# A planner that plays each candidate move forward before it orders TensorE's work

## The chip, the core and the metric

The kernel runs on one core of one Trainium2 chip. A core has engines that run their own instruction streams in order and wait for one another by semaphores: TensorE (PE in the profile; its weight loads are PEld), VectorE (DVE), ScalarE (ACT), GpSimd (POOL) and SyncE (SP, which here issues the DMA transfers). The metric is device time in microseconds (us). "The region" below always means the part of a run between value steps 16 and 448, a term explained with the kernel.

## What is computed

A gated attention block over 2048 tokens of width 640. The input is normalised, goes through attention with 32 heads of width 20, and through a two-layer ReLU network whose output, after a SiLU, gates the attention's output. The input is added at the end.

```python
xn = _layernorm(x, axis=-1)
qkv = (xn @ wqkv)                       # 32 heads, Dh = 20
scores = einsum("bhqd,bhkd->bhqk", q, k) * scale
p = softmax(scores, axis=-1)
s = (einsum("bhqk,bhkd->bhqd", p, v) merged) @ wo
g = silu(relu(xn @ w1) @ w2)
return x + s * g
```

All inputs and the output are fp32.

## The kernel before

**Order written at build time.** The kernel is built with a manual schedule: instructions run on each engine in the order in which the Python program emits them. A `Plan` object (L81 to L154) keeps a simulated clock in nanoseconds: `plan.t` for PE, `plan.free["act"]`, `plan.free["dve"]` and so on for the times at which the other engines come free, with fixed prices at the top of the file (`PAIR` 220 for a pair of score matmuls, `PV` 850 for a value step, `MM` 216 and `MM_HALF` 136 for filling, `EXP` 585, `RED` 605, `LAG` 210 from PE to a reader, `BACK` 120 back to PE). A loop at the end of the program (L1252 to L1301) looks at this clock, picks what PE does next, emits it with all that follows from it, and goes on. The simulated clock serves only to choose the order; the chip runs at its own pace.

**The attention.** Heads are taken four at a time (8 groups `g`), queries 512 at a time (4 columns `c`), keys 128 at a time (16 tiles `k`). That is 8 x 4 x 16 = 512 *value steps*. Work for them comes in units of one 128 x 512 block of scores of one head:

- A *maximum unit* (`mx_unit`, L617): a matmul with queries down the partitions (L629) into a PSUM bank, and a reduction on DVE (L633). After the 64 units of one `(g, c)`, `highest` (L640) and `rows` (L658) transpose the maxima on PE (L661), split them on DVE and send them through DRAM into two extra rows of the queries (`m_d`, one store and four loads on SP), which subtract the maximum inside the second score matmul.
- A *score unit* (`st_unit`, L719): a matmul with keys down the partitions (L732) and an exponential on ACT (L736) into one of three weight buffers (`ring`, `PTS` = 3, four units each).
- A *value step* (`weigh`, L764): when four score units are done, four heads' fp32 matmuls with the values (L772), side by side in PE's columns, into the bank `pv`. After 16 of them `normalise` (L780) copies `pv` out, transposes it on PE (L794), divides and stores it.

Contractions of the two score matmuls have 60 and 62 rows, so two units run side by side in PE's two half arrays: `pair` (L645) emits them two at a time, in the kinds score and maximum, two scores, or two maxima. Seven PSUM banks (`BANKS`) are shared by all this and the filling.

**The filling.** All other matrix products are cut into pieces that may go between: value projections, query and key projections of later heads, the hidden layer (`gate_hidden`, L846), the gate (`gate_out`, L917) and the first four fifths of the output projection (`out_first`, L1019). Each is a generator; `products` (L298) splits a contraction of 128 rows into two halves of 64 so that a filling piece uses the same half-array layout as the pairs (L314), with two accumulations at a time, each in its own bank. Between the two halves it waits until PE's order has read the earlier ones back (`plan.seen > last`). Filling pieces are 512 wide (L314 with tiles `xt`) or 320 wide (`w2`, `v` and `wo`).

Changing between the half-array layout ("A"), the value step's layout ("P") and the full array ("F") costs `SWITCH` in the plan.

**The choice before.** The loop takes the first that applies: a pair whose banks and operands are ready within `STAY`, and whose ACT or DVE queue is shorter than `FULL` (while in layout A) or `SOON` (otherwise), the neediest first; up to two value steps (`pv_count`), if no pair is coming, the queues are longer than `STOCK`, or PE isn't in layout A; a small task (the transposes of `rows` and `normalise`); a piece of the start-up chain (`first`); a piece of filling, if it is behind its pace or no pair is coming. `pace` (L1245) lets filling run `AHEAD` = 40000 ns ahead of a share of `FILLING` (the price of all filling but the output projection, 481 us in the plan's prices) in proportion to value steps done, and without limit after step 448. `mx_start` lets maxima run at most 64 + 160 units ahead of the scores' column.

Of the kernel before, what the change touches and what calls it, by code (L numbers as in the profile page):

```python
# [17 lines left out]
P = 128  # L18
# [7 lines left out]
NT = S // P  # L26
CW = 512
NC = S // CW
TPC = CW // P
NG = H // 4  # L30
# [4 lines left out]
PTS = 3  # L35
BANKS = 7
STEPS = NG * NC * NT
INF = float("inf")
# [10 lines left out]
EPS = 1e-5  # L49


SWITCH = 100
LAG = 210
BACK = 120
PAIR = 220
PV = 850
MM = 216
MM_HALF = 136
TURN = 110
EXP = 585  # L60
RED = 605
# [5 lines left out]
SLACK = 500  # L67
LEAN = 5000
XS = 12
SOON = 560  # L70
STAY = 60
FULL = 1300
MIXED = 400
STOCK = 900
AHEAD = 40000
OTS = 4
FILLING = NT * 15 * MM_HALF * 2 + (KD - 1) * NC * 30 * MM + NC * KF * 15 * MM + NT * 72 * MM_HALF
LEAD = 80


class Plan:  # L81
# [3 lines left out]
    def __init__(self):  # L85
        self.t = 0.0
        self.mode = None
        self.free = dict.fromkeys(("act", "dve", "pool", "dma", "sp"), 0.0)
        self.out = deque()
        self.events = []  # L90
        self.count = 0
        self.idle = 0.0
        self.switches = 0
        self.issued = 0
        self.seen = 0
        self.filled = 0.0
        self.jobs = []
        self.woken = 0.0

    def at(self, when, fn):  # L100
        heappush(self.events, (when, self.count, fn))
# [41 lines left out]
    def begin(self, mode, ready):  # L143
        return max(self.t + (SWITCH if mode != self.mode else 0), ready)

    def pe(self, mode, cost, ready=0.0):

        start = self.begin(mode, ready)
        self.switches += mode != self.mode
        self.idle += start - self.t - (SWITCH if mode != self.mode else 0)  # L150
        self.mode = mode
        self.issued += 1
        self.t = start + cost
        return self.t + LAG  # L154


@with_exitstack
def attention_gate(ctx: ExitStack, tc: tile.TileContext, x, wqkv, wo, w1, w2, out):
    nc = tc.nc
    ctx.enter_context(tc.manual_schedule())  # L160
    plan = Plan()
# [11 lines left out]
    pv = psum.tile([P, CW], F32, name="pv")  # L173
    banks = [psum.tile([P, CW], F32, name=f"ps{i}") for i in range(BANKS)]
    bank_free = [0.0] * BANKS
    behind = [0] * BANKS
# [5 lines left out]
    def take():  # L182

        i = min(range(BANKS), key=lambda i: bank_free[i])
        ready = bank_free[i]
        bank_free[i] = INF
        return i, ready
# [33 lines left out]
    small = []  # L221
# [76 lines left out]
    def products(ps, pairs, free):  # L298

        if st_done[0] == 0 or st_done[0] > 4 * (STEPS - 10):
            return (yield from whole(ps, pairs, free))
        cost = MM if ps[0].shape[-1] == CW else MM_HALF
        half = [slice(0, P // 2), slice(P // 2, P)]
        n = len(pairs[0])
        for second in range(2):
            for i in range(n):
                yield free  # L310
                for which in range(2):
                    rows = half[which ^ second]
                    a, b = pairs[which][i]
                    nc.tensor.matmul(ps[which], a[rows], b[rows],  # L314
                                     start=(i == 0 and not second), stop=(i == n - 1 and bool(second)))
                got = plan.pe("A", cost, free)
            if not second:
                last = plan.issued
                yield from when(lambda: plan.seen > last)
        return got  # L320

    def whole(ps, pairs, free):
# [8 lines left out]

    def take_two():
        (a, fa), (b, fb) = take(), take()
        return (a, b), max(fa, fb)


# [114 lines left out]
    def when(test):  # L451
        while not test():
            yield INF
# [33 lines left out]
    pack_ready = {}  # L487
# [98 lines left out]
    def v_tiles(n, t):  # L586
# [7 lines left out]
        for u, b in zip((t, t + 1), bs):  # L594
# [99 lines left out]
    st_done = [0]  # L694
    pts = {}
    pv_done = [0]
    pv_free = [0.0]
    pt_free = {}
    st_issued = {}
    p_ready = {}  # L700
# [5 lines left out]
    def where(step):  # L706
        return step // (NC * NT), step // NT % NC, step % NT
# [56 lines left out]
    def weigh():  # L764
        step = pv_done[0]
        g, c, k = where(step)
        pv_done[0] += 1
        pt = pts.pop(step)
        plan.seen = max(plan.seen, st_issued.pop(step))
        got = plan.pe("P", PV, max(p_ready.pop(step), pv_free[0] if k == 0 else 0))  # L770
        for h in range(4):
            nc.tensor.matmul(pv[32 * h:32 * h + DH + 1, :], va[g // 4][:, k, 4 * (g % 4) + h, :], pt[:, h, :],  # L772
                             start=(k == 0), stop=(k == NT - 1))
        pt_free[step] = plan.t + BACK
        if k == NT - 1:
            normalise(g, c, got)
# [309 lines left out]
    first = deque()  # L1086
    fill = deque()
# [73 lines left out]
    def values(n):  # L1161
        for t in range(0, NT, 2):
            yield from v_tiles(n, t)
        if n == 0:
            v_half(1)
        else:
            wvp.close()
# [34 lines left out]
    def ready_of(q, many=1):  # L1202


        best = INF, None
        n = 0
        for gen in list(q):
            at = head(q, gen)
            if at is None:
                continue  # L1210
            n += 1
            if at < best[0]:
                best = at, gen
            if best[0] <= plan.t + STAY or n == many:
                break
        return best

    def step_of(q, gen):
        del heads[gen]
        head(q, gen)  # L1220

    log = []

    def starving(engine):
        return plan.free[engine] - plan.t < SOON

# [18 lines left out]
    def pace():  # L1245
# [3 lines left out]
            return AHEAD + FILLING * (1 + n / ((NG - 1) * NC * NT))  # L1249
        return INF  # L1250

    while True:  # L1252
        plan.due()
        t = plan.t
        go = plan.begin("A", 0)
        options = choose(t)
        inside = plan.mode == "A"
        now = [o for o in options if o[0] <= go + STAY and o[1] < (FULL if inside else SOON)]
        if now:
            best = min(now, key=lambda o: (o[1] if len(set(o[2])) == 1 else o[1] - MIXED))  # L1260
            pair(best[2])
            log.append((t, "".join(best[2])))
            continue
        n = pv_count()
        coming = min([o[0] for o in options if o[1] < FULL], default=INF)
        if n and (coming == INF or min(plan.free["act"], plan.free["dve"]) - t > STOCK or plan.mode != "A"):
            for _ in range(n):
# [59 lines left out]
```

## Time and profile before

| | |
|---|---|
| time, median of 3 runs | 1788.44 us (1787.75 to 1790.27) |
| profiled execution | 1788.3 us |
| its span, first to last instruction | 1786.5 us |
| matmul instructions | 14887 |
| score units, maximum units | 2048 each |
| value matmuls (L772) | 4096, in 512 steps of eight |
| granted PE clock, mean | 0.992 |

Busy time of an engine is the union of its instructions' recorded times. Matmuls overlap in the records: a 512-wide one is recorded with some 0.38 us and the next may begin 0.06 or 0.22 us after it, so a busy PE isn't the same as a PE that does all it could. In the timeline the first column is the start, the second the length of a merged run of instructions, and "x16" how many were merged. A row of busy time in a stretch begins with the stretch and its length, then each engine's busy time and number of instructions, the granted PE clock, the DMA engines' share and GB/s; asked for a line or a tile, it holds that line's or tile's instructions alone. In the rows of waits come who waited, for whom, the total in us, how often, and the longest.

### The profile page before, as it was taken

Reading aid. Unit: us, or ns where it says so; the run is one execution under the profiler, and the core shown is the slowest. Engines: PE = TensorE matmul, PEld = TensorE weight load, DVE = VectorE, ACT = ScalarE, POOL = GpSimd, SP = SyncE. Lnnn points to the kernel's source line nnn. Section 1 sums busy time; section 2 is a strip of 40 time slices with the busy share of each in tenths; the row PEclk is TensorE's granted clock in tenths of the full one; section 3 lists DMA queues with packets and bytes.
Section 4 is the critical chain, followed back from the end, with each engine's and each line's share of the span. In section 5 each row is a group of like instructions: output and inputs, shape, how many; then the busy total and the mean of one; then the engine's idle time right before and its main releaser. Section 6 shows DMA issues by size and latency. Waiting matters only on the chain. (4 is left out here: it accounts for less than half of the span.)

```text
span 1786.5 us, 36686 instructions
## 1 busy us (share of the span) xinstructions
PE 1734.0 (97%) x14887; PEld 723.6 (41%) x14887; DVE 1451.6 (81%) x2512; ACT 1390.6 (78%) x2338; POOL 315.9 (18%) x338
## 2 busy tenths in 40 slices
PE   4999999999999999999999989999999999999998
PEld 3443334444332333444433324444444444344332
DVE  7699988888888888888888878888888888887522
ACT  3537788888888888887887868888788878887785
POOL 1631200002111455322221103000000000012221
PEclk8999999999999999999999999999999999999998
DMA  6324311201115332311112071131013100323332
GB/s 240 102 62 125 99 33 35 49 20 37 58 41 162 96 93 89 107 51 43 45 39 73 29 216 42 55 92 56 13 55 92 55 9 20 109 87 124 102 100 74
DMA packets 133995, 135.30 MB, mean 76 GB/s; under 512 B 26640, under 2 KB 110480, under 8 KB 133824
## 3 DMA queue, kind: packets, MB, share of 16 engines
q1 hardware_dynamic: 133248, 131.63, 24.4%
q8 instruction: 116, 1.90, 0.4%
q10 hardware_dynamic: 576, 1.31, 0.2%
q14 instruction: 55, 0.45, 0.1%
HBM read 85.32 MB, written 47.58 MB: 74 GB/s over the span
## 5 line engine op out<-in xcount | busy, mean ns | idle before, releaser
L736 ACT ACTIVATE pt<-ps,cexp 128x512 f32<-128x512 f32 x2048 | 1249.4, 689 | 293.0 <-PE ps L732 244.8
L633 DVE TENSOR_REDUCE m<-ps 128x1 f32<-128x512 f32 x2048 | 1274.4, 684 | 211.0 <-PE ps L629 204.6
L629 PE MATMUL ps<-kp,qp 60*128 60x512 f16 x2048 | 585.6, 378 | 5.3 <-ACT pt L736 3.7
L732 PE MATMUL ps<-qp,kp 62*128 62x512 f16 x2048 | 579.4, 379 | 9.3 <-DVE m L633 4.7
L772 PE MATMUL pv<-pt,va 128*21 128x512 f32 x4096 | 523.0, 600 | 0.0
L732 PEld LDWEIGHTS <-kp 62*128 62x128 f16 x2048 | 147.3, 93 | 332.2 <-issue 289.6
L629 PEld LDWEIGHTS <-qp 60*128 60x128 f16 x2048 | 150.1, 93 | 117.3 <-issue 84.7
L772 PEld LDWEIGHTS pv<-pt,va 128*21 128x21 f32 x4096 | 88.4, 100 | 237.3 <-issue 226.4
L1048 POOL TENSOR_TENSOR pre<-pre,go 128x320 f32<-128x320 f32 x32 | 27.0, 864 | 596.3 <-DVE go L1046 596.3
L314 PE MATMUL ps<-w2th,hh 64*128 64x320 f16 x768 | 126.5, 296 | 0.1
L314 PE MATMUL ps<-w2th,hl 64*128 64x320 f16 x768 | 126.0, 295 | 0.0
L314 PE MATMUL ps<-w2tl,hh 64*128 64x320 f16 x768 | 125.6, 295 | 0.0
L314 PEld LDWEIGHTS <-hh 64*128 64x128 f16 x1536 | 88.2, 94 | 51.2 <-issue 10.5
L314 PE MATMUL ps<-xt_hi,1h 64*128 64x512 f16 x480 | 102.7, 376 | 0.0
L314 PE MATMUL ps<-xt_lo,1h 64*128 64x512 f16 x480 | 102.1, 375 | 0.0
L314 PE MATMUL ps<-xt_hi,1l 64*128 64x512 f16 x480 | 100.3, 375 | 0.5 <-POOL 1l L287 0.5
L314 PEld LDWEIGHTS <-1h 64*128 64x128 f16 x960 | 58.7, 94 | 53.0 <-issue 18.7
L896 POOL CAST hh<-hr 128x512 f16<-128x512 f32 x48 | 29.3, 610 | 287.2 <-ACT hr L894 258.5
L482 POOL TENSOR_TENSOR loq<-rq,hiq 128x512 f16<-128x512 f32 x16 | 18.5, 1159 | 260.2 <-ACT rq L480 260.2
L314 PE MATMUL ps<-xt_hi,qh 64*128 64x512 f16 x150 | 56.4, 376 | 0.0
L314 PE MATMUL ps<-xt_lo,qh 64*128 64x512 f16 x150 | 56.4, 376 | 0.0
L898 POOL TENSOR_TENSOR hl<-hr,hh 128x512 f16<-128x512 f32 x48 | 55.7, 1160 | 3.8
(219 smaller groups left out, 1521.7 us busy)
## 6 DMA issues: line engine op xcount, KB each, us to landing
kp<-k_d SPq DMA_DIRECT2D x28, 240.0 KB
qp<-q_d SPq DMA_DIRECT2D x28, 240.0 KB
hh_d<-hh SPq DMA_DIRECT2D x48, 128.0 KB
hl_d<-hl SPq DMA_DIRECT2D x48, 128.0 KB
hh<-hh_d SPq DMA_DIRECT2D x8, 768.0 KB
hl<-hl_d SPq DMA_DIRECT2D x8, 768.0 KB
q_d<-hiq SPq DMA_DIRECT2D x20, 256.0 KB
k_d<-hik SPq DMA_DIRECT2D x20, 256.0 KB
```

Source lines behind the costliest of these rows:

```text
L314: nc.tensor.matmul(ps[which], a[rows], b[rows], start=(i == 0 and not second), stop=(i == n - 1 and bool(second)))
L482: nc.gpsimd.tensor_sub(lo, r, hi)
L629: nc.tensor.matmul(banks[b], qp[p % RING][r, t:t + P], kp[p % RING][r, kc * CW:(kc + 1) * CW], start=True, stop=True)
L633: nc.vector.tensor_reduce(m4[:, 2 * pr + j, qt, kc:kc + 1], banks[b], axis=AX.X, op=ALU.max)
L732: nc.tensor.matmul(banks[b], kp[p % RING][r, k * P:(k + 1) * P], qp[p % RING][r, c * CW:(c + 1) * CW], start=True, stop=True)
L736: exps[step, u] = nc.scalar.activation(pt[:, u, :], banks[b], AF.Exp, scale=cexp).ins
L772: nc.tensor.matmul(pv[32 * h:32 * h + DH + 1, :], va[g // 4][:, k, 4 * (g % 4) + h, :], pt[:, h, :], start=(k == 0), stop=(k == NT - 1))
L896: nc.gpsimd.tensor_copy(hi, r)
L898: nc.gpsimd.tensor_sub(lo, r, hi)
L1048: nc.gpsimd.tensor_add(pre[:, t, ns], pre[:, t, ns], gts[t][:, ns])
```

## The change

A class `Look` is added: a small copy of the plan's state (PE's time and layout, seven banks, ACT's and DVE's queues, counts of units and steps, the filling piece in hand), with the same prices. In the region, and while some scores and maxima are left (16 and 8 units at least), the loop no longer takes the first choice that applies:

- Small tasks and start-up pieces that are ready go first.
- Otherwise every possible move (`moves`) is tried on a copy, and the old rules (`go_on`) are played on from there; at 4, 5, ... 19 us after the decision the state is scored by `loss`, and the move with the smallest sum is emitted (`best`). Nothing is emitted during the trial.
- `loss` is PE time that did no matmul, a quadratic term for filling away from its target, and 100 ns for each unit by which the maxima's lead over the scores is below 140. The target has `AHEAD` as before; the quadratic term adds `BEHIND` = 60000 ns to the lag, so it is smallest where filling is 60 us below `target`.
- A value step is chosen one at a time. A chosen filling piece may wait up to 1 us for its operand; otherwise filling is not offered for 300 ns. Without any move the plan's clock goes 40 ns on.
- `products` and `take_two` note the filling piece in hand and its two banks, for `Look` to copy.

Before step 16 and after step 448 the old rules run. Two of their constants change, there and in the played moves: `SWITCH` 100 to 120, `SOON` 560 to 700.

```diff
-SWITCH = 100
+SWITCH = 120
...
-SOON = 560
+SOON = 700
...
+HELD = 1e15
+STOCKED = 0.0
+BEHIND = 60000
+FAR = 100
+WANT = 140
+HORIZON = 20000
+FROM = 4000
+SWAY = 2e5
...
+class Look:
...
+    def pe(self, mode, cost, ready):
+        self.t = max(self.t + (SWITCH if mode != self.mode else 0), ready) + cost
+        self.mode = mode
+        self.issued += 1
+        self.useful += cost
...
+    def moves(self):
+        t = self.t
+        res = [o[2] for o in self.options() if o[0] <= t + 300]
+        if self.values():
+            res.append("pv")
+        if self.fill_at() <= t + 300:
+            res.append("fill")
+        return res
+
+    def best(self):
+
+        moves = self.moves()
+        if not moves:
+            return None
+        found = None
+        for move in moves:
+            new = self.copy().make(move)
+            loss = 0
+            for end in range(FROM, HORIZON, 1000):
+                while new.t < self.t + end:
+                    new.go_on()
+                loss += new.loss(self)
+            if found is None or loss < found[0]:
+                found = loss, move
+        return found[1]
+
+    def loss(self, begun):
+        lag = self.filled - self.target(self) + BEHIND
+        return self.t - begun.t - (self.useful - begun.useful) + lag * lag / SWAY - STOCKED * (
+            min(self.act - self.t, 1200) + min(self.dve - self.t, 1200)) + FAR * max(0, WANT - (self.mx - self.st))
...
+    A_STEP = PV + 4 * PAIR
+
+    def target(at):
+
+        done = at.pv * PV + (at.st + at.mx) * PAIR / 2
+        return FILLING * min(1, done / ((NG - 1) * NC * NT * A_STEP)) + AHEAD
...
     while True:
         plan.due()
         t = plan.t
+        assert t < 3e6
+        if 16 <= pv_done[0] < 448 and st_done[0] < 4 * STEPS - 16 and mx_done[0] < len(mx_units) - 8:
+            urgent = [s for s in small if s[0] <= t + STAY]
+            if urgent:
+                small.remove(urgent[0])
+                urgent[0][2]()
+                log.append((t, "small"))
+                continue
+            (a, of_first), (b, of_fill) = ready_of(first, 8), ready_of(fill)
+            if a <= t + STAY:
+                step_of(first, of_first)
+                log.append((t, "first"))
+                continue
+            open_ = b < INF or (plan.part and plan.part["left"] == plan.part["half"])
+            move = look(bool(open_) and t >= blocked).best()
+            if move == "pv":
+                weigh()
+                log.append((t, "pv"))
+                continue
+            if move == "fill":
+                if b < t + 1000:
+                    if b > t:
+                        plan.idle += b - t
+                        plan.t = b
+                        plan.due()
+                    filled = plan.t
+                    step_of(fill, of_fill)
+                    plan.filled += plan.t - filled
+                    log.append((t, "fill"))
+                else:
+                    blocked = t + 300
+                continue
+            if move:
+                pair(("st",) * move[0] + ("mx",) * move[1])
+                log.append((t, "stst" if move[0] > 1 else "stmx" if move[0] else "mxmx"))
+                continue
+            plan.idle += 40
+            plan.t += 40
+            continue
```

`go_on` repeats the old choice step by step on the copy, `make` books a move's prices there, `values` tells how many value steps are ready (not counting whether the projected values are), and `look` copies the state from the plan.

More of the change, by code (lines that the diff above doesn't have):

```diff
@@ L98, in __init__ @@
         self.woken = 0.0
+        self.part = None
+        self.last_part = 15, MM
     def at(self, when, fn):
@@ L154, in pe, with copy, take, options @@
         return self.t + LAG
+class Look:
+    def copy(self):
+        new = Look.__new__(Look)
+        new.__dict__.update(self.__dict__)
+        new.free = self.free[:]
+        new.behind = self.behind[:]
+        new.steps = self.steps.copy()
+        return new
+    def take(self):
+        i = min(range(BANKS), key=self.free.__getitem__)
+        ready = self.free[i]
+        self.free[i] = HELD
+        return i, ready
+    def pe(self, mode, cost, ready):
[3 more added lines that the diff above has]
+        self.useful += cost
+    def options(self):
+        two = sorted(self.free)[1]
+        if two >= HELD:
+            return []
+        st = min(self.st_cap, 4 * (self.pv + PTS)) - self.st
+        mx = min(self.mx_cap, self.st // 64 * 64 + self.lead) - self.mx
+        act, dve = self.act - self.t, self.dve - self.t
+        res = []
+        if st > 0:
+            at = two if self.st < self.st_known else max(two, self.st_next)
+            if mx > 0:
+                res.append((at, max(act, dve), (1, 1)))
+            if st > 1:
+                res.append((at, act, (2, 0)))
+        if mx > 1:
+            res.append((two, dve, (0, 2)))
+        return res
+    def values(self):
+        n = 0
+        while n < 2:
+            step = self.pv + n
+            if 4 * step + 4 > self.st or n and step % NT == 0:
+                break
+            ready = max(self.steps[step][0], self.pv_free if step % NT == 0 else 0)
+            if ready > self.t + (SWITCH if self.mode != "P" else 0) + n * PV + STAY:
+                break
+            n += 1
+        return n
+    def fill_at(self):
+        if not self.can_fill:
+            return INF
+        if self.left == 0 and not self.reserve():
+            return INF
+        if self.left == self.half and not self.seen > self.last:
+            return INF
+        return max(self.t, self.part_free)
+    def reserve(self):
+        if sorted(self.free)[1] >= HELD:
+            return False
+        (a, ra), (b, rb) = self.take(), self.take()
+        self.held = a, b
+        self.part_free = max(ra, rb)
+        self.left = 2 * self.half
+        return True
+    def make(self, move):
+        if move == "pv":
+            ready, issued = self.steps.pop(self.pv)
+            self.seen = max(self.seen, issued)
+            self.pe("P", PV, max(ready, self.pv_free if self.pv % NT == 0 else 0))
+            self.pv += 1
+            if self.pv % NT == 0:
+                if self.act < self.dve:
+                    self.act = max(self.act, self.t + LAG) + 600
+                    self.pv_free = self.act + BACK
+                else:
+                    self.dve = max(self.dve, self.t + LAG) + 690
+                    self.pv_free = self.dve + BACK
+                self.dve += 740
+        elif move == "fill":
+            self.pe("A", self.cost, self.part_free)
+            self.filled += self.cost
+            self.left -= 1
+            if self.left == self.half:
+                self.last = self.issued
+            if self.left == 0:
+                for b in self.held:
+                    self.act = max(self.act, self.t + LAG) + self.evac
+                    self.free[b] = self.act + BACK
+        else:
+            ready = self.st_next if move[0] and self.st + move[0] > self.st_known else 0
+            (a, ra), (b, rb) = self.take(), self.take()
+            self.seen = max(self.seen, self.behind[a], self.behind[b])
+            self.pe("A", PAIR, max(ra, rb, ready))
+            got = self.t + LAG
+            for b, st in ((a, move[0] > 0), (b, move[0] > 1)):
+                if st:
+                    self.act = max(self.act, got) + EXP
+                    self.free[b] = self.act + BACK
+                    self.steps[self.st // 4] = self.free[b], self.issued
+                    self.st += 1
+                else:
+                    self.dve = max(self.dve, got) + RED
+                    self.free[b] = self.dve + BACK
+                    self.mx += 1
+                    if self.mx % 64 == 0:
+                        self.dve += 750
+                self.behind[b] = self.issued
+        return self
+    def go_on(self):
+        t = self.t
+        inside = self.mode == "A"
+        options = self.options()
+        go = t if inside else t + SWITCH
+        best = None
+        for o in options:
+            if o[0] <= go + STAY and o[1] < (FULL if inside else SOON):
+                want = o[1] - MIXED if o[2][0] == 1 else o[1]
+                if best is None or want < best[0]:
+                    best = want, o[2]
+        if best:
+            return self.make(best[1])
+        n = self.values()
+        coming = min([o[0] for o in options if o[1] < FULL], default=INF)
+        if n and (coming == INF or min(self.act, self.dve) - t > STOCK or not inside):
+            for _ in range(n):
+                self.make("pv")
+            return self
+        at = self.fill_at()
+        if at <= t + STAY and (self.filled < self.target(self) or coming > t + MM + 20):
+            return self.make("fill")
+        nxt = min(at, coming)
+        for o in options:
+            if o[1] >= FULL:
+                nxt = min(nxt, t + o[1] - FULL)
+        if self.pv in self.steps and 4 * self.pv + 4 <= self.st:
+            nxt = min(nxt, max(self.steps[self.pv][0], self.pv_free if self.pv % NT == 0 else 0) - STAY - SWITCH)
+        self.t = max(t + 20, nxt if nxt < HELD else t + 100)
+        return self
+    def moves(self):
+        t = self.t
+        res = [o[2] for o in self.options() if o[0] <= t + 300]
[3 more added lines that the diff above has]
+            res.append("fill")
+        return res
+    def best(self):
[17 more added lines that the diff above has]
+            min(self.act - self.t, 1200) + min(self.dve - self.t, 1200)) + FAR * max(0, WANT - (self.mx - self.st))
@@ L307, in products @@
         n = len(pairs[0])
+        plan.part = part = dict(left=2 * n, half=n, last=0, cost=cost, free=free, banks=plan.taken)
         for second in range(2):
@@ L316, in products @@
                 got = plan.pe("A", cost, free)
+                part["left"] -= 1
             if not second:
-                last = plan.issued
+                part["last"] = last = plan.issued
                 yield from when(lambda: plan.seen > last)
+        plan.part, plan.last_part = None, (n, cost)
         return got
@@ L333, in take_two @@
         (a, fa), (b, fb) = take(), take()
+        plan.taken = a, b
         return (a, b), max(fa, fb)
@@ L1250, in pace, with look @@
         return INF
+    A_STEP = PV + 4 * PAIR
+    def target(at):
+        done = at.pv * PV + (at.st + at.mx) * PAIR / 2
+        return FILLING * min(1, done / ((NG - 1) * NC * NT * A_STEP)) + AHEAD
+    def look(can_fill):
+        now = Look()
+        now.t, now.mode = plan.t, plan.mode
+        now.free = [min(f, HELD) for f in bank_free]
+        now.behind = behind[:]
+        now.act, now.dve = plan.free["act"], plan.free["dve"]
+        now.st, now.mx, now.pv = st_done[0], mx_done[0], pv_done[0]
+        now.steps = {k: (p_ready[k], st_issued[k]) for k in range(pv_done[0], (st_done[0] + 3) // 4)}
+        now.pv_free = pv_free[0]
+        now.issued, now.seen = plan.issued, plan.seen
+        now.useful = 0.0
+        now.filled = plan.filled
+        now.target = target
+        now.can_fill = can_fill
+        part = plan.part
+        now.left, now.half, now.cost, now.last, now.part_free = (
+            (part["left"], part["half"], part["cost"], part["last"], part["free"]) if part else (0,) + plan.last_part + (0, 0))
+        now.held = part["banks"] if part else ()
+        now.evac = 480
+        now.lead = 64 + 2 * LEAD
+        now.st_known = now.st_cap = st_done[0]
+        now.st_next = 0.0
+        for n in range(1, 33):
+            unit = st_done[0] + n - 1
+            g, c, k = where(unit // 4)
+            if unit >= 4 * STEPS or (g, c) not in q_ready:
+                break
+            now.st_cap = unit + 1
+            if q_ready[g, c] <= plan.t:
+                now.st_known = unit + 1
+            else:
+                now.st_next = q_ready[g, c]
+        now.mx_cap = mx_done[0]
+        for n in range(1, 41):
+            if mx_done[0] + n > len(mx_units):
+                break
+            g, c, kc, qt, pr, j = mx_units[mx_done[0] + n - 1]
+            p = 2 * g + pr
+            if max(pack_ready.get((p, "k", kc * CW), INF), pack_ready.get((p, "q", c * CW), INF)) > plan.t:
+                break
+            now.mx_cap = mx_done[0] + n
+        return now
+    blocked = 0.0
     while True:
@@ L1254, in attention_gate @@
         t = plan.t
+        assert t < 3e6
[13 more added lines that the diff above has]
+            move = look(bool(open_) and t >= blocked).best()
+            if move == "pv":
+                weigh()
[11 more added lines that the diff above has]
+                    log.append((t, "fill"))
+                else:
+                    blocked = t + 300
[7 more added lines that the diff above has]
+            continue
         go = plan.begin("A", 0)
```

## The prediction

> **What bounds the kernel now.** I read the page's busy table first, then the timeline of PE over 10 us, then busy time by source line in chosen stretches, and last who waited for whom.
>
> ```profile
> span 1786.5 us, 36686 instructions
> PE 1734.0 (97%) x14887; PEld 723.6 (41%) x14887; DVE 1451.6 (81%) x2512; ACT 1390.6 (78%) x2338; POOL 315.9 (18%) x338
> ```
>
> PE looks full, which would leave the change some 3%. But the busy time of pipelined matmuls overlaps and hides gaps, so I rebuild PE's load from distances between starts.
>
> ```profile
> 1251.38 1.91 PE L772 MATMUL pv<-pt,va 128*21 128x512 f32 x16
> 1253.23 0.39 PE L732 MATMUL ps<-qp,kp 62*128 62x512 f16 x2
> 1253.45 0.38 PE L629 MATMUL ps<-kp,qp 60*128 60x512 f16 x2
> 1253.77 1.06 PE L772 MATMUL pv<-pt,va 128*21 128x512 f32 x8
> 1254.76 0.39 PE L732 MATMUL ps<-qp,kp 62*128 62x512 f16 x1
> ...
> 1258.65 0.33 PE L314 MATMUL ps<-w2th,hh 64*128 64x320 f16 x2
> 1258.79 0.32 PE L314 MATMUL ps<-w2tl,hh 64*128 64x320 f16 x2
> ```
>
> The reader sees four prices. A pair of 512-wide half-array matmuls lasts 0.216 us (1253.23 to 1253.45 shows 0.22), a 320-wide pair 0.136 (1258.65 to 1258.79). One value step is eight L772 matmuls in fours: two steps take 1.85 and one 0.99, so a step is 0.86 (0.43 per four) and leaving the value matmuls costs 0.13. Entering them costs 0.32 - 0.22 = 0.10. A visit to the value matmuls thus loses 0.23 us, however many steps it holds.
>
> The change acts between value steps 16 and 448. These rows are the busy time of that region, 172 to 1573 us, by source line: L772, L732, L629, L314, then the transposes L794 and L661, then the PE work on tiles xt_hi and xt_lo; the last row is a group of the whole run, one of three forms for the values.
>
> ```profile
> 172.00:1573.00 1401.00, 436.35 (x3460) 74.56 (x3456) 1.00 0.22 66
> 172.00:1573.00 1401.00, 503.67 (x1731) 128.56 (x1731) 1.00 0.22 66
> 172.00:1573.00 1401.00, 527.11 (x1815) 135.60 (x1815) 1.00 0.22 66
> 172.00:1573.00 1401.00, 663.24 (x5112) 298.60 (x5114) 1.00 0.22 66
> 172.00:1573.00 1401.00, 17.70 (x108) 11.34 (x108) 1.00 0.22 66
> 172.00:1573.00 1401.00, 7.87 (x28) 2.44 (x28) 1.00 0.22 66
> 172.00:1573.00 1401.00, 326.76 (x1806) 1.00 0.22 66
> 172.00:1573.00 1401.00, 186.49 (x904) 1.00 0.22 66
> L314 PE MATMUL ps<-vh,xt_hi 64*128 64x320 f16 x160 | 28.4, 296 | 0.2 <-ACT pt L736 0.2
> ```
>
> Value steps: 3460 / 4 x 0.43 = 372 us. Score pairs: (1731 + 1815) / 2 x 0.216 = 383. Of L314's 5112, the 512-wide ones use xt: 1806 + 904, less 3 x 160 for the values (320-wide), leaves 2230, or 1115 pairs x 0.216 = 241; the other 2882 are 1441 pairs x 0.136 = 196. Transposes: at most 26. **PE's real load is 1218 us of 1401; 183 us are lost.**
>
> ```profile
> 186.93 1.92 PE L772 MATMUL pv<-pt,va 128*21 128x512 f32 x16
> ...
> 1571.65 1.06 PE L772 MATMUL pv<-pt,va 128*21 128x512 f32 x8
> ```
>
> These are the first and last of the 308 value visits in the region: 308 x 0.23 = 71 us. The 28 + 108 / 4 = 55 transpose visits lose about 2 x 0.10 each (estimated by the entry price): 11. The remaining 183 - 82 = 101 us are waits for a bank or an operand. Are ACT and DVE full instead?
>
> ```profile
> DVE m L633 <- PE ps L629: 172.0, 234, 2.6
> ACT pt L736 <- PE ps L732: 203.3, 146, 3.3
> 1045.55 4.73 ACT L736 ACTIVATE pt<-ps,cexp 128x512 f32<-128x512 f32 x8 [0.26 <-PE ps L629]
> 1045.58 3.68 DVE L633 TENSOR_REDUCE m<-ps 128x1 f32<-128x512 f32 x6
> L736 ACT ACTIVATE pt<-ps,cexp 128x512 f32<-128x512 f32 x2048 | 1249.4, 689 | 293.0 <-PE ps L732 244.8
> L633 DVE TENSOR_REDUCE m<-ps 128x1 f32<-128x512 f32 x2048 | 1274.4, 684 | 211.0 <-PE ps L629 204.6
> 172.00:1573.00 1401.00, 1385.41 (x12279) 580.10 (x12277) 1200.94 (x2040) 1136.04 (x1906) 214.53 (x227) 1.00 0.22 66
> ```
>
> No: in the region DVE waits 172 us for PE's maxima and ACT 203 us for its scores; DVE is busy 1201 us (86%) and ACT 1136 (81%). All three have gaps because of the order in which PE does things: PE bounds, through its order.
>
> **The change, part by part.** No matmul, exponential, reduction or transfer of data is added or taken away; each still executes once. What moves is PE's order, and with it the order on ACT, DVE and SP. The planning runs before the kernel does and costs the chip nothing.
>
> *The look-ahead.* From step 16 to 448 each move (a pair of either kind, a value step, a filling piece, or a small task first) is chosen by playing about 20 us on. The score is lost PE time, so both kinds of loss above are charged. Its prices are near the chip's: a pair 220 ns (0.216), a value step 850 (0.86), a switch now 120 (0.10 and 0.13), an exponential 585 against (4.73 - 0.69) / 7 = 577, a reduction 605 against (3.68 - 0.68) / 5 = 600 (0.69 and 0.68 are the recorded mean lengths, taken off for the last one of the run). So what it saves on paper should mostly be saved on the chip.
>
> *Waits.* The bound is 0 to 101 us. For a value in between I ask what the present order reaches where filling is plentiful and in short pieces, and where it has none. First 1100 to 1400 us, then 1030 to 1090; in each the lines L772, L732, L629, L314.
>
> ```profile
> 1100.00:1400.00 300.00, 94.91 (x768) 16.59 (x768) 1.00 0.21 55
> 1100.00:1400.00 300.00, 106.80 (x382) 28.00 (x382) 1.00 0.21 55
> 1100.00:1400.00 300.00, 109.94 (x396) 29.03 (x394) 1.00 0.21 55
> 1100.00:1400.00 300.00, 149.35 (x1456) 83.09 (x1456) 1.00 0.21 55
> ...
> 1030.00:1090.00 60.00, 19.39 (x136) 3.20 (x136) 0.94 0.63 185
> 1030.00:1090.00 60.00, 19.85 (x68) 5.20 (x69) 0.94 0.63 185
> 1030.00:1090.00 60.00, 19.09 (x64) 4.79 (x63) 0.94 0.63 185
> 1030.00:1090.00 60.00, 16.14 (x152) 8.70 (x152) 0.94 0.63 185
> ```
>
> The good stretch (all of its L314 320-wide): 82.6 + 84.0 + 99.0, with transposes at the region's rate 271 of 300, 0.903; the region as a whole has 1218 / 1401 = 0.869. The hole, between the last hidden-layer piece and the gate weights: 14.6 + 14.3 + 10.3 + 1 = 40 of 60, 0.67, and the granted clock falls to 0.94. I take it that the look-ahead holds 0.903 throughout, except in the hole, whose cause (loads) it does not touch: 1218 / 0.903 = 1349, which is 52 us less; the hole keeps (54 - 40) / 0.903 = 15 of them. **Waits and uneven stretches: -37 us.**
>
> *Fewer visits.* 432 steps in 308 visits is 1.4 each; the three-deep ring of weights allows pairs, 216 visits. Bounds 0 and 92 x 0.23 = 21 us. I take half: **-10 us.**
>
> *Filling.* The old pace lets filling run 40 us ahead of the attention's progress; the new one aims 60 us lower (40000 - 60000), so the gate's last pieces and the output projection end later, in the last stretch.
>
> ```profile
> L314 PEld LDWEIGHTS <-qh x300: 91/94/97, 127.8 to 543.9; 64*128 64x128 f16 x150
> ```
>
> The projections that later heads wait for are filling too. Their last piece runs at 544 us; 60 us later is still early, as group 6, the first to need it, begins at step 384, near 172 + 368 / 432 x 1401 = 1365 us. So nothing starves, PE's load only changes place, and I take 0; both ends are in the slower rival.
>
> *SWITCH, SOON outside the region*, 172 us before and 214 after: the old rules with other constants. I take 0, bounds ±2% of 386, about ±8 us.
>
> *Small tasks first.* The 55 transpose visits now go ahead of pairs and value steps and bring their DVE work and SP transfers along (the maxima's store and four loads back, or the store of outputs). The next column's exponentials wait for those loads, but the look-ahead is charged when maxima are fewer than 140 units ahead, some 140 x 0.6 = 84 us of DVE. What can change is whether a visit joins another: ±55 x 0.10 = ±6 us. I take 0. No instruction gets a wait that it did not have.
>
> Sum: -37 - 10 = -47 us. The profiled execution took 1788.3 us (its span of 1786.5 and 1.8 around it), 0.1 under the median; 1788.3 - 47, rounded, is **1741 us**.
>
> [...]
>
> **The rivals.**
>
> *Evacuation binds (0.17).* Seven banks and two engines at 86% and 81% keep PE waiting whatever the order; only visits are saved, and a few waits. For it: in the hole, with no filling on PE, ACT and DVE run 4.7 and 3.7 us without a gap (the rows at 1045.55 and 1045.58). Against it: 172 and 203 us of waits for PE. It gives -5 to -25, in the middle **1773 us**. [...]
>
> *The order does not hold on the chip (0.07).* A tightly packed order has no slack, and each late bank or DMA stalls all behind it in PE's fixed order, so the gain goes: **1788 us**, within 4.
>
> *Filling pushed into the end (0.10), slower.* After step 448 there are few maxima left, and the region cannot shrink by what it hands over if DVE (1201 us busy) then sets its length. If the last stretch grows by the full 60 us and the region comes down by only 40, to 1361, where DVE would be at 88%, the sum is +20: **1808 us**. It decides once the region saves less than the filling time moved out of it. Against it: those 214 us have gaps of their own.
>
> ```profile
> 1573.00:1787.00 214.00, 202.46 (x1694) 77.85 (x1690) 112.48 (x199) 162.77 (x274) 47.19 (x56) 0.98 0.29 96
> ```
>
> ACT is busy 163 of 214 and DVE 112 there.
>
> **How the numbers follow.** The forecast has 0.66 and its own range 1708 to 1766: its upper end keeps the visits and a third of the 37 (-22); its lower end adds half of the other 64 us of waits (-79 in all, rounded up). With the rivals, 0.17 + 0.66 = 0.83 are faster by over 0.2% (3.6 us, about what a measurement of this kernel can tell from no change), 0.07 the same, 0.10 slower. The range runs from 1700 (0.05 left below it) to 1790, takes in the rival of no change but for its upper edge (0.02), and leaves out the slower one: 0.17 in all.
>
> **What the profile after would show.** Right: L772 visits in the region well under 308; DVE's and ACT's waits for PE under 172 and 203 us; real PE load 0.90 or more of a region near 1350 us; w2's L314 pieces still running after value step 448, and a last stretch longer than 214. Wrong: the same visits and waits; DVE above 95%, which is the evacuation rival; a last stretch that grows by more than the region shrinks; or more stretches at a granted clock below 1, as in the hole.

## The result and the profile after

The changed kernel takes 1761.43 us (median of 4 runs, 1760.59 to 1762.05) beside 1789.07 us of the kernel before: a ratio of 0.9845, 95% interval 0.9828 to 0.9862, or 27.6 us less. The forecast was 1741. One execution of the experiment e1_constants below, the profiled one, took 3156.4 us at a mean granted clock of 0.898; it is left out of e1's time, and of its profile only the number of visits is used, which the order fixes at build time.

The head of the page of the changed kernel, and its matmuls with w2, the last filling before the output projection, from the view of the filling's line (its line numbers are higher by 195 to 198: L509 is the old L314, L827 L629, L831 L633, L930 L732, L934 L736, L970 L772):

```profile
span 1760.3 us, 36592 instructions
...
PE 1712.6 (97%) x14839; PEld 686.8 (39%) x14839; DVE 1455.5 (83%) x2510; ACT 1408.9 (80%) x2340; POOL 316.1 (18%) x338
...
L509 PE MATMUL ps<-w2tl,hh x768: 293/295/471, 1029.2 to 1517.0; 64*128 64x320 f16 x192
```

PE is "97% busy" after as before, with 26 us gone: the row was blind to what changed. (It counts 48 matmuls fewer: of the output projection, 96 half-array matmuls of L509 ran as 48 on the full array at L525, as `products` does once the scores of all but the last ten steps are done. The prediction said that no matmul is added or taken away; it is off by these.)

The same sum as in the prediction, for the region after, 170 to 1551 us: busy time by line, in the order L970, L930, L827, L509, L992, L859, then the tiles xt_hi and xt_lo.

```profile
170.00:1551.00 1381.00, 453.67 (x3460) 62.69 (x3456) 1.00 0.23 67
170.00:1551.00 1381.00, 497.77 (x1730) 121.00 (x1732) 1.00 0.23 67
170.00:1551.00 1381.00, 509.71 (x1800) 127.00 (x1800) 1.00 0.23 67
170.00:1551.00 1381.00, 652.05 (x5130) 293.77 (x5130) 1.00 0.23 67
170.00:1551.00 1381.00, 17.68 (x108) 11.32 (x108) 1.00 0.23 67
170.00:1551.00 1381.00, 7.76 (x28) 2.45 (x28) 1.00 0.23 67
170.00:1551.00 1381.00, 318.21 (x1820) 1.00 0.23 67
170.00:1551.00 1381.00, 183.50 (x910) 1.00 0.23 67
```

Value steps 3460 / 4 x 0.43 = 372; pairs 1765 x 0.216 = 381; filling (1820 + 910 - 480) / 2 = 1125 x 0.216 = 243, and 1440 x 0.136 = 196; transposes 25. That is 1217 us of 1381, a load of 0.881 against 0.869, and 164 us lost against 183.

What is lost has changed its kind. The timeline of PE in the same stretch as before:

```profile
1257.19 1.05 PE L970 MATMUL pv<-pt,va 128*21 128x512 f32 x8
1258.17 0.31 PE L509 MATMUL ps<-w2th,hl 64*128 64x320 f16 x2
...
1258.54 0.38 PE L827 MATMUL ps<-kp,qp 60*128 60x512 f16 x1
1258.95 1.06 PE L970 MATMUL pv<-pt,va 128*21 128x512 f32 x8
...
1261.06 1.06 PE L970 MATMUL pv<-pt,va 128*21 128x512 f32 x8
```

One step ("x8") at a time. A visit still costs 0.98 - 0.86 = 0.12 to leave (1257.19 to 1258.17), but there are now 415 visits in the region where there were 308, and 485 against 378 in the whole run. The region's first and last:

```profile
180.55 1.06 PE L970 MATMUL pv<-pt,va 128*21 128x512 f32 x8
...
1549.10 1.92 PE L970 MATMUL pv<-pt,va 128*21 128x512 f32 x16
```

At 0.23 us they lose 95 us against 71. So the rest of the loss, with the transposes' 11 in it, fell from 183 - 71 = 112 to 164 - 95 = 69. Booking each distance between two starts, less the matmul's own slot, on what comes next, the waits in front of score pairs within the half-array layout sum to about 45 us before and to none after. The engines behind PE say the same; waits in the region after:

```profile
DVE m L831 <- PE ps L827: 142.5, 317, 3.4
ACT pt L934 <- PE ps L827: 127.8, 247, 2.7
ACT pt L934 <- PE ps L930: 82.4, 144, 3.9
```

DVE waits 143 us for PE against 172, ACT 210 against 203 + 40 = 243, and in more and shorter waits: 317 times for DVE's against 234 (0.45 us on average against 0.74).

The stretch that the prediction took as its anchor did not get fuller. These are the lines L970, L930, L827 and L509 after, from 1085 to 1385 us, all of L509 320-wide:

```profile
1085.00:1385.00 300.00, 103.17 (x792) 14.59 (x792) 1.00 0.21 55
1085.00:1385.00 300.00, 101.41 (x390) 25.29 (x389) 1.00 0.21 55
1085.00:1385.00 300.00, 101.86 (x390) 26.14 (x390) 1.00 0.21 55
1085.00:1385.00 300.00, 140.72 (x1416) 77.78 (x1414) 1.00 0.21 55
```

That is 85.1 + 84.2 + 96.3 and some 5 of transposes, 271 of 300 or 0.90 as before, with 93 visits where there were 65. The gain lies elsewhere: cut into eighths by value steps, the region loses, visits and waits together, 28, 22, 24, 19, 32, 20, 17 and 21 us before, and 21, 21, 22, 17, 32, 17, 16 and 21 after. The eighth with the hole, the fifth, is unchanged.

### The profile page after: what moved, and what is told of

Its sections match the earlier page's. It is cut to its first block, busy times and chain, and to the rows that moved or that the text cites. A ratio compares the mean times of both kernels' runs of the same rounds, so it can differ in the third digit from the quotient of the medians.

```text
span 1760.3 us, 36592 instructions
## 1 busy us (share of the span) xinstructions
PE 1712.6 (97%) x14839; PEld 686.8 (39%) x14839; DVE 1455.5 (83%) x2510; ACT 1408.9 (80%) x2340; POOL 316.1 (18%) x338
## 5 line engine op out<-in xcount | busy, mean ns | idle before, releaser
L934 ACT ACTIVATE pt<-ps,cexp 128x512 f32<-128x512 f32 x2048 | 1266.6, 688 | 255.6 <-PE ps L827 131.7
L831 DVE TENSOR_REDUCE m<-ps 128x1 f32<-128x512 f32 x2048 | 1281.4, 684 | 183.2 <-PE ps L827 171.5
L930 PE MATMUL ps<-qp,kp 62*128 62x512 f16 x2048 | 571.2, 380 | 4.3 <-ACT pt L934 1.6
L827 PE MATMUL ps<-kp,qp 60*128 60x512 f16 x2048 | 568.5, 379 | 3.0 <-ACT pt L934 1.9
L970 PE MATMUL pv<-pt,va 128*21 128x512 f32 x4096 | 537.9, 599 | 0.1
L930 PEld LDWEIGHTS <-kp 62*128 62x128 f16 x2048 | 139.6, 93 | 406.6 <-issue 365.3
L827 PEld LDWEIGHTS <-qp 60*128 60x128 f16 x2048 | 141.9, 94 | 85.3 <-issue 50.0
L970 PEld LDWEIGHTS pv<-pt,va 128*21 128x21 f32 x4096 | 76.2, 99 | 198.1 <-issue 189.7
L509 PE MATMUL ps<-w2th,hl 64*128 64x320 f16 x768 | 124.7, 297 | 2.0 <-DMA hl<-hl_d 2.0
L509 PE MATMUL ps<-w2th,hh 64*128 64x320 f16 x768 | 124.9, 297 | 0.6 <-DMA hh<-hh_d 0.6
L509 PE MATMUL ps<-w2tl,hh 64*128 64x320 f16 x768 | 124.4, 297 | 0.0
L509 PEld LDWEIGHTS <-hh 64*128 64x128 f16 x1536 | 85.8, 94 | 47.5 <-issue 7.1
L509 PE MATMUL ps<-xt_hi,1h 64*128 64x512 f16 x480 | 100.2, 375 | 0.0
L509 PE MATMUL ps<-xt_hi,1l 64*128 64x512 f16 x480 | 100.1, 375 | 0.0
L509 PE MATMUL ps<-xt_lo,1h 64*128 64x512 f16 x480 | 99.7, 375 | 0.0
L509 PEld LDWEIGHTS <-1h 64*128 64x128 f16 x960 | 59.7, 94 | 48.8 <-issue 13.9
L509 PE MATMUL ps<-xt_lo,qh 64*128 64x512 f16 x150 | 56.3, 375 | 0.0
L509 PE MATMUL ps<-xt_lo,kh 64*128 64x512 f16 x150 | 56.3, 375 | 0.0
L509 PE MATMUL ps<-xt_hi,qh 64*128 64x512 f16 x150 | 56.3, 375 | 0.0
```

What stands on the lines that cost most here:

```text
L509: nc.tensor.matmul(ps[which], a[rows], b[rows], start=(i == 0 and not second), stop=(i == n - 1 and bool(second)))
L827: nc.tensor.matmul(banks[b], qp[p % RING][r, t:t + P], kp[p % RING][r, kc * CW:(kc + 1) * CW], start=True, stop=True)
L831: nc.vector.tensor_reduce(m4[:, 2 * pr + j, qt, kc:kc + 1], banks[b], axis=AX.X, op=ALU.max)
L930: nc.tensor.matmul(banks[b], kp[p % RING][r, k * P:(k + 1) * P], qp[p % RING][r, c * CW:(c + 1) * CW], start=True, stop=True)
L934: exps[step, u] = nc.scalar.activation(pt[:, u, :], banks[b], AF.Exp, scale=cexp).ins
```

## The experiments

Twelve kernels ran, each timed against the kernel before on its chip (1789.5 to 1789.6 us there). The table takes the time from each kernel's median and the rest from the profiled executions of the two kernels and six of the twelve. *Load* is the sum of all matmul slots (from all starts, so it differs by 1 to 3 us from the sums above); *visits* are to the value matmuls; *rest* is what is lost besides them; the last stretch runs from step 448 to the start of the last matmul.

| kernel | time, us | region | its load | visits (x 0.23) | rest | last stretch | its load |
|---|---|---|---|---|---|---|---|
| before | 1789 | 1401 | 1215 | 308 (71) | 115 | 207 | 164 |
| e7_nudge | 1797 | 1414 | 1218 | 303 (70) | 126 | 203 | 161 |
| e9_constants_nudge | 1783 | 1401 | 1216 | 305 (70) | 115 | 203 | 165 |
| after | 1761 | 1381 | 1214 | 415 (95) | 71 | 201 | 167 |
| e2_look_only | 1777 | 1394 | 1224 | 405 (93) | 77 | 199 | 155 |
| e3_both_steps | 1783 | 1410 | 1238 | 359 (83) | 89 | 196 | 144 |
| e4_no_behind | 1853 | 1482 | 1242 | 398 (92) | 149 | 192 | 140 |
| e12_two_deep | 1754 | 1374 | 1214 | 396 (91) | 69 | 199 | 165 |

### The change taken apart: constants and look-ahead

e1 is the kernel before with the constants of the change, e2 the changed kernel with those of before:

```diff
-SWITCH = 100
+SWITCH = 120
...
-SOON = 560
+SOON = 700
```

```diff
-SWITCH = 120
+SWITCH = 100
...
-SOON = 700
+SOON = 560
```

> The kernel before with only the two constants of the change: SWITCH 120 and SOON 700, no look-ahead. Theory A (the chosen order of the look-ahead brings the gain, the constants hardly any): 1789, within 5 us. Rival B (the constants bring it: prices nearer to the chip's): 1762 to 1775. The visits to the value matmuls stay near 378 by either.

> The changed kernel with SWITCH and SOON put back to 100 and 560: the look-ahead alone. Theory A: 1761, within 6 us. Rival B: back towards 1780 to 1789. Visits near 475 of 512 steps by A, since single value steps come from the look-ahead and not from the price of a switch.

e1 took 1776.3 us, 0.9924 (0.9907 to 0.9940); e2 1776.9, 0.9925 (0.9911 to 0.9940). Neither theory holds: the constants alone take 13.4 us (the 12.8 in the expectations below counts the long execution), the look-ahead alone 12.8, and together they take 27.6. A's part about the visits held: they stay at 373 with the constants and rise to 475 with the look-ahead.

### Is that more than the scatter of orders?

Half a gain from two constants of a plan asks for caution: any change of a price gives another order. So the constants ran singly, and each corner ran again with a price moved by 1 ns, which means nothing.

```diff
-SWITCH = 100
+SWITCH = 120      # e5_switch_only, on the kernel before
...
-SOON = 560
+SOON = 700        # e6_soon_only, on the kernel before
...
-BACK = 120
+BACK = 121        # e7_nudge on the kernel before, e9 on e1, e10 on the changed kernel, e11 on e2
```

> The kernel before with SWITCH 120 alone (SOON stays 560). Both constants together took 12.8 us. Theory F (a plan whose switch price is nearer to the 0.10 + 0.13 us of the trace keeps step with the chip): 1776 to 1783. Rival G (any small shift of the plan's prices gives another order, and orders scatter by some 10 us): anywhere from 1778 to 1798, and the nudged kernel of the same batch moves as much.

> The kernel before with SOON 700 alone (SWITCH stays 100). Theory F: it does nothing by itself, 1790 within 5 us. Rival G: as far off as e5, either way. Third possibility: the whole 12.8 us is SOON's, 1777.

> The kernel before with BACK 121 in place of 120: one nanosecond on one price of the plan, with no meaning of its own. It measures how far two orders of the same rules lie apart. Theory F: within 5 us of 1790. Rival G: 8 us or more away.

> The kernel before with SWITCH 120 and SOON 700, and BACK 121 in place of 120. Without the nudge the two constants took 12.8 us, though one alone gave 0 and the other +6. If the pair has a real effect: 1772 to 1781. If that order was a lucky draw of the scatter that the nudge of the kernel before showed (7 us): 1783 to 1797.

> The changed kernel with BACK 121. If its 27.6 us stand apart from the scatter of orders: 1757 to 1769. If the changed kernel is itself a lucky draw: 1770 to 1780.

> The changed kernel with SWITCH 100 and SOON 560 and BACK 121. Without the nudge 1776.9. Look-ahead alone, if the right constants belong to it: 1772 to 1782 again. If 1776.9 was an unlucky draw and the constants do not matter to it: 1760 to 1768.

e5: 1790.3, 1.0006 (0.9996 to 1.0015). e6: 1795.9, 1.0041 (1.0026 to 1.0056). e7: 1796.9, 1.0044 (1.0027 to 1.0061), so **one nanosecond on one price costs 7 us**, just short of rival G's 8. Theory F falls with e5 and e6: neither constant brings its gain alone, and e6 leaves F's 5 us. e9: 1782.9, 0.9965 (0.9952 to 0.9978). e10: 1764.2, 0.9860 (0.9845 to 0.9874). e11: 1775.7, 0.9925 (0.9909 to 0.9942). The last two fell in the ranges for an effect apart from the scatter. With each corner as the mean of its two draws:

| | SWITCH 100, SOON 560 | SWITCH 120, SOON 700 | constants |
|---|---|---|---|
| old rules | (1789.5 + 1796.9) / 2 = 1793.2 | (1776.3 + 1782.9) / 2 = 1779.6 | -13.6 |
| look-ahead | (1776.9 + 1775.7) / 2 = 1776.3 | (1761.4 + 1764.2) / 2 = 1762.8 | -13.5 |
| look-ahead's part | -16.9 | -16.8 | |

The two parts add up, and both exceed the scatter, which is 6 to 7 us between draws of the old rules and 1 to 3 with the look-ahead. e9 fell at the edge between its two expectations, and lies only 6.6 us below the kernel before, no more than the scatter; with the pair of draws on either side I count the constants' effect as real, if only by two draws. Singly they do nothing (e5, e6: 3 us to either side of 1793). **Why the two are worth 13 us together and nothing alone stays open.** Under the look-ahead the table gives part of it: from e2 to after, 10 of the 13 us of the region are load, filling that the changed kernel leaves for the last stretch. Under the old rules it depends on the draw: from e7 to e9 the load is the same and the waits fall by 11, but from the kernel before to e9 the region does not change at all (1401 us, 115 of the rest), and the gain is before and after it.

### The price of a switch

> The changed kernel with SWITCH 110, between the old price and the new one, near the mean of 0.10 and 0.13 us. If the look-ahead's gain hangs on the right price: 1755 to 1762. If the higher price as such helps, by making value visits dearer: 1765 to 1772, half way to the 1777 at 100 (with SOON 560).

The edit is SWITCH 110 in the changed kernel. It took 1765.4, 0.9869 (0.9854 to 0.9883), at the lower edge of "half way" and 3.4 us above its upper edge for the right price. Given the draws above it says no more than that 120 is not critical.

### Are the added visits a mere loss?

```diff
-            new = self.copy().make(move)
+            new = self.copy()
+            for _ in range(new.values() if move == "pv" else 1):
+                new.make(move)
...
-            move = look(bool(open_) and t >= blocked).best()
+            now = look(bool(open_) and t >= blocked)
+            move = now.best()
             if move == "pv":
-                weigh()
...
+                n = now.values()
+                for _ in range(n):
+                    weigh()
```

> The changed kernel, but a value move takes both value steps when two are ready, in the played moves and in what is emitted. The changed kernel makes 485 visits against 378 before, and a visit loses 0.23 us. Theory C (the added visits are pure loss which the look-ahead fails to see): visits fall and each saves 0.23 us, 1745 to 1752. Theory D (single steps are the price of the shorter waits: a double step of 1.85 us empties the banks in front of ACT and DVE): the waits come back by as much or more, 1760 to 1772.

1782.9, 0.9958 (0.9942 to 0.9975): 21 us slower than the changed kernel, and beyond what theory D asked for. The visits in the region fall from 415 to 359, which saves 13 us, and the rest of the loss rises from 71 to 89, 18 us. So far D holds: single visits buy shorter waits. In the region of e3 (its lines are higher by 2) DVE waits 170 us for PE against 143, ACT 229 against 210:

```profile
DVE m L833 <- PE ps L829: 169.5, 313, 2.9
ACT pt L936 <- PE ps L829: 147.2, 192, 8.5
ACT pt L936 <- PE ps L932: 82.0, 131, 3.9
```

But that is 5 or 6 of the 21. The rest is in the filling; these are the filling's lines in the region of e3, then in its last stretch and in that of the changed kernel:

```profile
170.00:1580.00 1410.00, 691.57 (x5414) 311.60 (x5414) 1.00 0.24 70
...
1580.00:1783.00 203.00, 40.08 (x388) 20.77 (x388) 0.97 0.23 75
```

```profile
1551.00:1761.00 210.00, 52.60 (x528) 27.43 (x528) 0.99 0.31 100
```

284 more filling matmuls run in the region (5414 against 5130), 142 pairs at 0.136 or 19 us, and with 24 more transposes of the output projection (36 against 12) the region's load is some 23 us higher. The last stretch, 23 us lighter, is only 5 us shorter in the table. **Work taken out of the last stretch is repaid there with a fifth to a third of its time**, 5 us for 23 in e3: over the look-ahead kernels of the table its load runs from 140 to 167 and its length from 192 to 201, 9 us for 27. With few maxima left, its length seems set by something other than PE's load; ACT is busy 163 of those 210 us:

```profile
1551.00:1761.00 210.00, 199.09 (x1668) 78.74 (x1666) 121.84 (x214) 163.12 (x274) 48.87 (x58) 0.99 0.31 100
```

Which wait it is was not tried.

### Does the filling's place matter?

```diff
-BEHIND = 60000
+BEHIND = 0
```

> The changed kernel with BEHIND 0 in place of 60000: filling is aimed 40 us ahead of the attention's progress, as the old pace had it. My prediction took the place of the filling to be worth nothing: 1761, within 8 us. Rival E (filling must be kept in stock so that each gap has a piece to put in; run ahead, it meets the holes between its phases early and is missing later): slower than 1775, perhaps slower than the kernel before.

1853.3, 1.0352 (1.0337 to 1.0368): 92 us slower than the changed kernel and 64 slower than the kernel before. My step "0" falls. Rival E gave the right sign, but its mechanism is the smaller part. By the table, the region is 101 us longer: 28 of load (filling out of the last stretch, which gets 9 shorter for it) and 78 more of waits, already in the early stretches, with filling left: in the first eighth of the region's value steps 35 us are lost against 21 in the changed kernel. DVE's and ACT's waits in the region of e4:

```profile
DVE m L831 <- PE ps L827: 215.9, 354, 3.1
ACT pt L934 <- PE ps L930: 179.3, 233, 9.8
ACT pt L934 <- PE ps L827: 137.0, 224, 3.8
```

Its timeline of PE shows what the waits look like at their start:

```profile
705.37 0.38 PE L930 MATMUL ps<-qp,kp 62*128 62x512 f16 x1
705.52 0.37 PE L827 MATMUL ps<-kp,qp 60*128 60x512 f16 x1
705.59 0.52 PE L509 MATMUL ps<-xt_hi,1h 64*128 64x512 f16 x2
705.95 0.38 PE L930 MATMUL ps<-qp,kp 62*128 62x512 f16 x1
706.10 0.37 PE L827 MATMUL ps<-kp,qp 60*128 60x512 f16 x1
706.17 0.52 PE L509 MATMUL ps<-xt_lo,1h 64*128 64x512 f16 x2
706.53 0.38 PE L930 MATMUL ps<-qp,kp 62*128 62x512 f16 x1
```

One pair and one filling piece every 0.58 us, the pace of ACT (seven exponentials in 4.16 us from 704.20, the last at the recorded mean of 0.69: (4.16 - 0.69) / 6 = 0.58), where PE needs 2 x 0.216 = 0.43: as I read these rows, the banks come free at ACT's pace, PE loses 0.15 us at each pair, and though a piece is open, no second one goes in. In the code there is a gate for that: the played rules fill only while `filled < target`, or while no pair is coming. With BEHIND 60000 the loss holds filling well under the target and the gate stays open; with 0 the loss is smallest right at the gate. That the gate does it is argued from these rows and the code; a kernel without it was not tried.

### Looking deeper

```diff
-            new = self.copy().make(move)
+            first = self.copy().make(move)
+            seconds = first.moves() or [None]
+            for second in seconds + [None]:
+                new = first.copy()
+                if second is not None:
+                    new.make(second)
...
-SWITCH = 120
+SWITCH = 115
-SOON = 700
+SOON = 850
-BEHIND = 60000
-FAR = 100
+BEHIND = 65000
+FAR = 50
-HORIZON = 20000
-FROM = 4000
+HORIZON = 25000
+FROM = 3000
```

> The changed kernel looking deeper: each first move is tried with each second move after it, 25 us on, the loss from 3 us, with SWITCH 115, SOON 850, BEHIND 65000 and FAR 50. If the rest of the waits is due to the short sight of the choice: 1740 to 1752. If it lies in what the choice cannot reach (seven banks, the hole without filling, the 0.23 us of a visit): 1754 to 1763.

**1753.6 us, 0.9802 (0.9787 to 0.9816): faster than both kernels**, 7.9 us under the changed one, and just below the lower edge of the second expectation. No nudged copy of it ran, so its 7.9 us stand against a scatter of 1 to 3 us that only other look-ahead kernels showed. In the region it makes 19 visits fewer (4 us) with 2 us less of the rest; DVE's waits go on falling (L836 and L832 are L831 and L827 of the changed kernel):

```profile
DVE m L836 <- PE ps L832: 136.8, 263, 1.9
```

Since search and constants moved together, their shares are not known. That 160 us stay lost in the region, 91 of them at visits, speaks for the limits named there.

## Why the prediction was right or wrong

*The bound: right.* PE's order, not the work of any engine, held the time. The rebuilt load found 183 us lost where the busy row (1385 of 1401) left 16, and the 20 us by which the region shrank are more than that row allowed. The other 8 of the 27.6 lie outside the region: 2 in the start-up and 6 in the last stretch. DVE rose only from 86% to 1199 / 1381 = 87% of the region.

*Waits, -37: about right.* They fell by 112 - 69 = 43. Pair waits within the layout vanished (about 45 us to none); the hole stayed, as assumed (a granted clock of 0.94 again, from 1020 to 1080 us). But the anchor, a good stretch's load everywhere, was not reached: the region's load came to 0.881 of 1381 us where 0.90 of some 1350 was forecast, since what the waits gave up went in part into visits.

*Fewer visits, -10: wrong in sign.* This is the step that failed. I took the price of a visit, 0.23 us, as a reason for the look-ahead to make fewer; it made 107 more in the region, +25 us. e3 shows that it pays: forcing doubles gave back 18 us of waits for 13 of visits, with longer waits of DVE and ACT for PE. That a single step of 0.99 us starves them less than a double one of 1.85 us is the likely reason. The two terms hang together, and I had added them as if they did not.

*SWITCH and SOON, 0 ± 8: wrongly confined.* I priced them only outside the region, where 8 us went, the edge of the bounds. Inside, they are part of the played rules, and I gave them no term there. In all they are worth 13 us of the 27.6, in two draws each. The look-ahead alone is worth 17, not 47. By the table the region moved by -44 for the rest and +24 for visits, -20 in all, where -47 was forecast. That the total still fell inside the range, at -27.6, is in part luck: one term had the wrong sign, and another was missing.

*Filling, 0: wrong twice.* It did not end later: w2's last piece runs at 1517 us, 34 before the region's end, where it was 43 before: 9 us later by that measure, where the aim had moved by 60. And its place is not neutral: e4 loses 92 us, and e3 shows that filling left for the last stretch adds a fifth to a third of its load to the time there; that the same load adds its whole length in the region is argued, not shown. The slower rival had this the wrong way round; in e4 what slows the kernel is filling aimed too early.

*The prices fit the chip: open.* No run sets the gain on the plan's clock beside the one on the chip. What the runs show is how sensitive orders are: one nanosecond gave 7 us (e7).

*Evacuation binds, 1773:* not what happened, as DVE and ACT still wait 143 and 210 us for PE. *The order does not hold on the chip, 1788:* no.

*Small tasks first, 0 ± 6:* not tried by itself.

## What to carry to other kernels

Before crediting a scheduling idea with a few microseconds, run the same rules with a meaningless nudge, since two orders of one rule lay 7 us apart here. Judge a packed engine by distances between starts (PE's busy row read 97% before and after, with 26 us gone), and price a layout change together with the queues that it empties: in e3, fewer and longer visits saved 13 us and cost 18 in other waits. In these kernels, work that can run at any time was cheapest in the last stretch (5 us for 23 of load in e3), where PE has gaps anyway (a load of 167 us in 201 after the change). A scoring rule whose optimum lies on a gate of the rules that it plays is worth a test of its own; here the gate is argued from the code, not tried.

## What the runs showed of the hardware that was not expected

In the hole of the kernel before, the granted clock was halved twice: it was 0.51 in the 3.40 us from 1039.10 and 0.50 in the 3.40 us from 1049.40. In the stretches just ahead, at a clock of 1.00, PE stood idle for 0.34 and 0.33 us. Busy time by stretch in the kernel before (PE, PEld, DVE, ACT, POOL, then the clock):

```profile
1035.70:1039.10 3.40, 3.06 (x13) 0.83 (x10) 3.35 (x6) 3.38 (x6) 0.00 (x0) 1.00 1.04 365
1039.10:1042.50 3.40, 3.40 (x15) 0.75 (x16) 3.35 (x6) 1.98 (x4) 0.00 (x0) 0.51 1.07 366
1042.50:1045.90 3.40, 3.40 (x29) 0.67 (x22) 1.60 (x3) 1.61 (x3) 0.00 (x0) 0.99 1.08 355
1045.90:1049.40 3.50, 3.17 (x12) 0.83 (x10) 3.47 (x7) 3.50 (x7) 0.00 (x0) 1.00 1.20 294
1049.40:1052.80 3.40, 3.40 (x18) 0.61 (x17) 1.78 (x5) 0.88 (x2) 0.00 (x0) 0.50 1.20 290
```

The stretches ahead of the two, 3.40 and 3.50 us long, hold 13 and 12 matmuls and are 90% and 91% busy by their rows; the 3.40 us from 1042.50 hold 29, and the stretch after them ran at 1.00. What lowered the clock these rows do not show, and no run was made to find it. The hole thus held, beside its waits, twice 3.40 us at about half the clock (0.51 and 0.50).
